# Diagonal blocks of a delta-rule inverse: copied by ScalarE in the first chunk, turned on chip instead of through DRAM in the second

## The chip, the cores and the metric

The kernel runs on one core of a Trainium2 chip. A core has five engines that run side by side, each with its own list of instructions in a fixed order: TensorE (PE in the profile; its weight loads are PEld), VectorE (DVE), ScalarE (ACT), GpSimd (POOL) and SyncE (SP), which here only issues DMA transfers. Engines wait for one another through semaphores. Work tiles lie in an on-chip memory of 128 partitions; TensorE writes its results to eight accumulator banks, and another engine has to copy them out before a bank can be used again. The metric is the time of one execution on the device in microseconds (us).

## The reference

Two blocks are computed one after the other. The first is a delta rule over a sequence, for 4 batches and 8 heads of 768 tokens with a head size of 48: a state matrix is read by each query and then corrected by each key. The second is a feed-forward layer with a SiLU.

```python
k_n = k / (norm(k) + 1e-6)
for t in range(S):                       # S = 768, per batch and head
    y[t] = q[t] @ state                  # state is 48 x 48
    v_old = k_n[t] @ state
    state = state + beta[t] * outer(k_n[t], v[t] - v_old)
x = y as (3072 tokens, 384)
out = silu(x @ w_in) @ w_out             # 384 -> 2048 -> 384
```

## The kernel before

**Chunks.** The 768 tokens are cut into six chunks of 128. Within a chunk the corrections depend on one another through the products of keys with keys. The kernel solves this triangular system by an inverse: the scores (key by key products, tile `ap`) are made by TensorE in `score`; their 32x32 diagonal blocks (four row groups of 32 tokens, 32 batch-head pairs) are brought into a layout where every partition holds one whole block, are inverted there by VectorE step by step (`invert_first` for chunk 0, `invert` for the others, which yield after each rank step), and the inverted blocks are joined to 64x64 ones by small matmuls (`joins` with `corner`, `turned`, `straight` and `merge_half` for chunk 0; `merge` for the others). Then `keys`, `inner`, `old`, `update` and `new` carry the state over the chunk and give the outputs, `hidden` and `combine` (or `project` for chunk 0) are the feed-forward layer.

**How the blocks get into that layout.** Three things have to be there before an inverse starts: the blocks, turned, in a tile `g`; a start value `x`; and a step size for each token, the product of beta and the squared inverse key norm with a minus sign, turned in the same way (`step`).
- Chunk 0: `diagonal_blocks` (line 1304) copies the 32x32 blocks out of the scores into the tile `stage`, eight copies of 32 partitions by 512 numbers, four for each pair of batches g; six are by GpSimd, two by ScalarE (lines 1324 and 1327). VectorE then turns all of them with one transpose (line 1353). The step sizes come out of `norm_steps` (line 395) on VectorE, which turns them with one small transpose as well.
- Chunk 1: `block_out` (line 578) writes the blocks to DRAM, four DMAs for each pair of batches, and `block_in` (line 589) reads them back in the turned layout with one DMA. The step sizes go through a sparse tile `spread` that four VectorE instructions fill (line 430); `block_steps` (line 450) turns it with a matmul on TensorE, and ScalarE copies the result out.
- Chunks 2 to 5 go as chunk 1.

**What sets the order.** No scheduler reorders anything: `pin` ties every instruction behind the one before it on the same engine, in the order of the program text, and `in_line` does this for the DMAs on SP. For chunk 0 the text itself is the order: key turns and scores (`first_score`), block copies, `beta_of(0)` (beta turned by TensorE, copied by ScalarE), query turns (`turn`, whose copies `kq` ScalarE makes), `norm_steps(0)`, query scores (`first_queries`), and filler matmuls (`busy`, line 347) in between, some of which wait for a rank step of the inverse. From the second half of chunk 0's joins on a string of letters is the order (`script`): `r` runs a piece of the feed-forward layer, `s` a step of the solving chain, `l` a step of chunk 1's key lengths, `norm_steps(1)` included, `p` a step of `prepare(1)` (scores and blocks of chunk 1), `g` the step sizes of chunk 1 and the start of its inverse, `i` a rank step, `f` a step of converting weights. Accumulator banks are handed out in three rotating groups, so the order also sets who waits for which bank.

Of the kernel before, what the change touches and what calls it, by code (L numbers as in the profile page):

```python
# [19 lines left out]
def kernel(  # L20
# [374 lines left out]
    def norm_steps(c):  # L395

        seed, t, r = (small.tile([P, BH], kind, name=name, bufs=1)[:] for name, kind in (
            ("seed", U32), ("nt", FP32), ("nr", FP32)
        ))
        ss = sums.pop(c)  # L400
        n = small.tile([P, BH], FP32, name="n", bufs=1)
        by_slot = small.tile([P, 2, B * NP], FP32, name="n_slot", bufs=1)
        yield pin(nc.vector.tensor_scalar(
            out=seed, in0=ss.bitcast(U32), scalar1=-0.5, scalar2=1597463007.0,
            op0=ALU.mult, op1=ALU.add,
        ))
        root = seed.bitcast(FP32)
        for _ in range(3):
            yield pin(nc.vector.scalar_tensor_tensor(
                out=t, in0=ss, scalar=-0.5, in1=root, op0=ALU.mult, op1=ALU.mult  # L410
            ))
            yield pin(nc.vector.tensor_tensor(out=t, in0=t, in1=root, op=ALU.mult))
# [7 lines left out]
        yield pin(nc.vector.tensor_tensor(out=t, in0=r, in1=beta_tok[:, c, :], op=ALU.mult))  # L420
        if c == 0:
            size = small.tile([P, T], FP32, name="step")
            pin(nc.vector.scalar_tensor_tensor(
                out=t, in0=r, scalar=-1.0, in1=t, op0=ALU.mult, op1=ALU.mult
            ))
            pin(nc.vector.transpose(out=size[:], in_=t))
            step_of[0] = size
        for j in range(NB if c > 0 else 0):
            rows = slice(T * j, T * (j + 1))
            yield pin(nc.vector.scalar_tensor_tensor(  # L430
                out=spread[rows, place(c, j), :], in0=r[rows], scalar=-1.0, in1=t[rows],
                op0=ALU.mult, op1=ALU.mult,
            ))
# [123 lines left out]
    def by_pool(to, of):  # L557
        return pin(nc.gpsimd.tensor_copy(out=to, in_=of))  # L558

    blocks = {}  # L560

    def block_room(c):

        if c == 0:
            g, x = (sum_room[:, at : at + T * T] for at in (AT_G, AT_X))
        else:
            g = work.tile([P, T * T], FP32, name="g", tag="g", bufs=1)[:]
            x = (
                sum_room[:, AT_LAST : AT_LAST + T * T] if c == 1
                else work.tile([P, T * T], FP32, name="x", tag="x", bufs=1)[:]  # L570
            )
        pin(nc.gpsimd.memset(x, 0.0))
# [3 lines left out]
        blocks[c] = (tc.dram_tile([P, T, T], FP32, name=f"blocks{c}") if c > 0 else None, g, x)  # L576

    def block_out(c, g):

# [719 lines left out]

        score(0, b, (0,), (A, CC), evacuate)  # L1300

    diagonal = stage[:, 0 : BH * T].rearrange("p (n t) -> p n t", t=T)

    def diagonal_blocks(g, engines):

        for j, by in enumerate(engines):
            rows, cols = slice(T * j, T * (j + 1)), slice(T * (j % 2), T * (j % 2 + 1))
            by(diagonal[rows, HH * g : HH * (g + 1)], aps[0, g][0][rows].rearrange("s u h t -> s (u h) t")[:, :, cols])

    load_q(0, slice(HB, B))  # L1310
    busy(3)
    for b in range(B):
# [32 lines left out]
    for _ in norm_steps(0):  # L1345
# [7 lines left out]
    pin(nc.vector.transpose(  # L1353
        out=blocks[0][1].rearrange("p s t -> p t s"), in_=diagonal.rearrange("p n t -> p t n")
    ))
    for t in xis:
        pin(nc.gpsimd.memset(t, 0.0))
    for c in range(1, NCH):
# [110 lines left out]
    def prepare(c):  # L1469

        def evacuate(j, e, to, of):
            if j == 1:
                mask(to, of)
            else:
                by_act(to, of)

        def scored(b):
            if b == 0:
                block_room(c)
            score(c, b, (0, 1), (A, CC), evacuate)  # L1480
            if b % HB == 1:
                block_out(c, b // HB)

        if in_blocks(c):
            for g in range(2):
                size(c, g)
            if c == 2:
                for b in range(B):
                    turn(c, b, 0, (A, CC)[b % 2], True)
            for g in range(2):  # L1490
                for b in range(HB * g, HB * (g + 1)):
                    turn_blocks(c, b, 1)
                if g == 1:
                    for b in range(HB):
                        scored(b)
                yield
            for b in range(HB, B):
                scored(b)
            block_in(c)
            yield  # L1500
            return
        block_room(1)
        for b in range(B):
            score(1, b, (0,), (CC, CC), evacuate)
# [25 lines left out]
    def script(text):  # L1530

        nonlocal pieces
        for word in text.split():
# [18 lines left out]
            elif what == "p":  # L1552
                go(ready, n)
            elif what == "w":
                paced(fetch_w_out, n)
            elif what == "W":
                paced(fetch_w_in, n)
            elif what == "Q":
                paced(load_q, 1)
            elif what == "o":  # L1560
                busy(n)
            elif what == "u":
                busy(n, wide=NARROW)
            elif what == "h":
                size_half(1, pins[seen_on])
            elif what == "v":
                paced(load_v, 1)
            elif what == "k":
                load_k(2)
            elif what == "g":  # L1570
                step = block_steps(1)
                pin(nc.gpsimd.memset(spread[:], 0.0))
                later["inv"] = invert(1, step)
            elif what == "i":
                go(later["inv"], n)
            elif what == "d":
                flush()
            elif what == "V":
                load_v(2)
            elif what == "G":  # L1580
                load_blocks(q, 2, slice(HB, B))
            elif what == "z":
                size(1, sizes_1.pop(0))
            elif what == "t":
                until(("out", NWI - 1))
                go(sums_made, n)
            elif what == "m":
# [5 lines left out]
    for text in (  # L1593
        "s f3 s q q s j32 b j20 r f j8 q f j4 f j16 r j44 b j4 q j4 r f r j22 f j12 f j8 f b j8 f j4 r j20 e r f j99 h f r f2 l s l r l p r l f p l s l2 f r3 l3 p l s l4 p l2 s r l f l4 f l f l2 p l s l2 s p f r f r l r l2 g i p l p f i p f l i r2 i r v f i3 r3 i r i r i3 b r2 f2 r2 i r2 i2 r2 i f b i r i3 f2 r2 f r3 f i2 r f i f r3 f r f i f i2 r i r i k i2 b z r2 i r i r z r i r2 b r t s r b r f s r2 t s m r m t2 r b m f t m s f b r m2 b m f s r m r s m4 s m3 c m4 s r t G m r2 m4 V m s r m r m t2",
    ):
        script(text)
    for c in range(1, NCH):
# [62 lines left out]
```

## Time and profile before

| | |
|---|---|
| median of 3 runs | 640.37 us (639.87 to 640.62) |
| the profiled execution | 638.56 us, of which the span from first to last instruction is 636.8 |
| busy share of the span: TensorE, VectorE, ScalarE, GpSimd | 97%, 63%, 34%, 15% |
| granted TensorE clock, mean over the span | 0.989 |
| SP's block writes of chunk 1 (issues) | 73.4 to 83.0 us |
| start of the inverse: chunk 0, chunk 1 | 20.0 us, 92.2 us |

Rows of the timeline begin with the start in us from the beginning of the span and the duration in us; then come engine, line, operation, what is written and what is read, with shapes and a count of merged instructions. In square brackets stands the idle time of the engine just before, and what ended it. Rows of a table of stretches give for each stretch its length, each engine's busy time with the number of its instructions, then the granted TensorE clock, the share of the DMA engines that was busy, and GB/s. A row of a DMA queue gives packets, MB and the share of 16 engines' time.

### The profile page before, as it was taken

To read this page: it belongs to the slowest core of one execution; us is meant where nothing else is said; L and a number is where in the kernel's file an instruction comes from. 1 tells how busy PE (TensorE), PEld (TensorE's weight loads), DVE (VectorE), ACT (ScalarE), POOL (GpSimd) and SP (SyncE) were. 2 spreads that over 40 slices of the span, in tenths; PEclk is the share of its full clock that TensorE was granted. 3 is DMA by queue.
4 is the path that set the end of the run, shared out by engine and by line. 5 is a ranking of instruction groups with operands and counts; after the bars stand their busy time and mean duration, and the time that the engine had idled before them with its cause. 6 is when DMAs were issued, how large, how long until landed. Compare 5 with 4: busy or idle time off the path is not lost.

```text
span 636.8 us, 21379 instructions
## 1 busy us (share of the span) xinstructions
PE 620.8 (97%) x9406; PEld 545.9 (86%) x9406; DVE 398.3 (63%) x901; ACT 216.1 (34%) x502; POOL 94.7 (15%) x104
## 2 busy tenths in 40 slices
PE   7879989999999999999999999999999999999997
PEld 5578778666799989989989989989989989889997
DVE  6986779999667974537974546974455964112112
ACT  4457663432441112541122541112451122441110
POOL 6224721335020020020020020020002000000000
PEclk9959999999999999999999999999999999999999
DMA  9646626350459360559150469150353133010101
GB/s 174 132 130 190 202 66 149 107 93 3 100 100 183 63 108 4 110 92 192 26 103 9 97 119 169 35 100 13 75 108 74 26 75 36 18 37 1 26 0 26
DMA packets 141308, 53.65 MB, mean 84 GB/s; under 512 B 112912, under 2 KB 134672, under 8 KB 141216
## 3 DMA queue, kind: packets, MB, share of 16 engines
q1 hardware_dynamic: 140880, 52.14, 39.8%
q8 instruction: 74, 1.21, 0.9%
q10 hardware_dynamic: 336, 0.15, 0.1%
q14 instruction: 18, 0.15, 0.1%
HBM read 39.62 MB, written 10.49 MB: 79 GB/s over the span
## 4 chain that ended last, share of the span: by engine, by line
PE 94%; DVE 3%; issue 1%; DMA 1%; ACT 0%; SPq 0%; POOL 0%; POOLq 0%; DVEq 0%
PE phid L1052 40%; PE px L1169 17%; PE py L1169 13%; PE po L1096 5%; PE pb_c L846 3%; PE pa L537 3%; PE pb_c L834 2%; PE pyc L925 2%; PE pb_c L1096 2%; PE pb_c L866 2%; PE pyc L912 1%; PE px L788 1%; PE py L788 1%; PE pb_c L537 1%; PE pt L508 1%
## 5 line engine op out<-in xcount | busy, mean ns | idle before, releaser
L1052 PE MATMUL phid<-xT,w_in 128*128 128x256 f32 x1152 | 257.1, 381 | 0.2 <-DVE xT L899 0.2
L1052 PEld LDWEIGHTS phid<-xT,w_in 128*128 128x128 f32 x1152 | 216.4, 190 | 30.2 <-issue 0.9
L1062 ACT ACTIVATE gT<-phid 128x512 f32<-128x512 f32 x88 | 52.5, 597 | 145.4 <-PE phid L1052 140.8
L1150 DVE TENSOR_TENSOR sums_of_g<-gT 128x384 f32<-128x384 f32 (+1 forms) x60 | 30.2, 526 | 65.2 <-ACT gT L1062 54.8
L636 DVE SCALAR_TENSOR_TENSOR rank<-g,step,x 128x31 f32<-128x31 f32 (+15 forms) x124 | 49.8, 402 | 22.3 <-DMA g<-blocks 18.8
L1169 PE MATMUL px<-sums_of_w,sums_of_g 128*128 128x192 f32 x320 | 56.6, 329 | 0.0
L1169 PE MATMUL py<-w_out,sums_of_g 128*128 128x192 f32 x320 | 56.2, 328 | 0.0
L1169 PEld LDWEIGHTS py<-w_out,sums_of_g 128*128 128x128 f32 x320 | 52.3, 190 | 0.3
L1169 PEld LDWEIGHTS px<-sums_of_w,sums_of_g 128*128 128x128 f32 x320 | 52.2, 190 | 0.4
L641 DVE TENSOR_TENSOR x<-x,rank 128x31 f32<-128x31 f32 (+15 forms) x124 | 42.5, 343 | 4.3
L475 POOL TENSOR_TENSOR vf<-vf,n_slot 128x768 f32<-128x768 f32 x10 | 14.8, 1493 | 175.5 <-DMA vf<-in_v_dram 175.4
L552 ACT COPY xT<-pyc 48x128 f32<-48x128 f32 (+2 forms) x126 | 32.8, 260 | 1.7
L496 DVE STREAM_TRANSPOSE kq<-stage 128x512 f32<-128x512 f32 x28 | 28.3, 1113 | 4.2 <-DMA xT<-part 2.4
L1169 PE MATMUL py<-w_out,gT 128*128 128x192 f32 x160 | 28.9, 330 | 0.0
L1180 DVE TENSOR_TENSOR o<-o,kept 128x192 f32<-128x192 f32 (+1 forms) x29 | 11.4, 420 | 26.6 <-ACT kept L1177 26.6
L1169 PE MATMUL px<-w_out,gT 128*128 128x192 f32 x160 | 27.9, 327 | 0.0
L1169 PE MATMUL px<-sums_of_w,gT 128*128 128x192 f32 x160 | 27.8, 327 | 0.0
L558 POOL COPY g<-x 64x256 f32<-64x256 f32 x4 | 5.0, 1241 | 150.2 <-DVE x L644 150.2
L1169 PEld LDWEIGHTS px<-w_out,gT 128*128 128x128 f32 x160 | 26.5, 190 | 0.6
L871 DVE TENSOR_TENSOR state<-state,pb_c 128x384 f32<-128x384 f32 x22 | 11.2, 550 | 25.0 <-PE pb_c L866 24.9
L1169 PEld LDWEIGHTS py<-w_out,gT 128*128 128x128 f32 x160 | 26.0, 190 | 0.4
L1169 PEld LDWEIGHTS px<-sums_of_w,gT 128*128 128x128 f32 x160 | 26.2, 190 | 0.1
(228 smaller groups left out, 936.1 us busy)
## 6 DMA issues: line engine op xcount, KB each, us to landing
vf<-in_v_dram SPq DMA_DIRECT2D x48, 96.0 KB, 2.9
out_dram<-o SPq DMA_DIRECT2D x42, 96.0 KB, 2.2
w_out<-in_moe_w_in_dram SPq DMA_DIRECT2D x4, 768.0 KB, 4.9
sums_of_w<-in_moe_w_out_dram SPq DMA_DIRECT2D x4, 768.0 KB, 5.4
blocks<-ap SPq DMA_DIRECT2D x40, 64.0 KB, 1.9
g<-blocks SPq DMA_DIRECT2D x5, 512.0 KB, 3.9
kb<-in_k_dram SPq DMA_DIRECT2D x12, 192.0 KB, 4.3
kb<-in_k_dram SPq DMA_DIRECT2D x24, 96.0 KB, 4.0
```

The costliest lines, as they stand in the source:

```text
L475: pin(nc.gpsimd.tensor_tensor(out=vf, in0=vf, in1=of, op=ALU.mult))
L496: pin(nc.vector.transpose(out=kqs[c, b][:, :, j, :].rearrange("p a (i m) -> p a m i", i=T), in_=src.rearrange("p a (m d) -> p a m d", d=D) ...
L537: pin(nc.tensor.matmul(pa[e][half, p * n * W : (p + 1) * n * W], lhsT=kq[rows, p, 0, half], rhs=kq[rows, p, js[0] : js[-1] + 1, half], sta ...
L552: return pin(nc.scalar.copy(to, of))
L636: pin(nc.vector.scalar_tensor_tensor(out=tv, in0=g[:, 0:m, m : m + 1].to_broadcast([P, m, n]), scalar=step[:, m : m + 1], in1=x[:, m : m + ...
L641: yield pin(nc.vector.tensor_tensor(out=x[:, 0:m, m:T], in0=x[:, 0:m, m:T], in1=tv, op=ALU.add))
L846: yield pin(nc.tensor.matmul(pz[rows, n * D : (n + 1) * D], lhsT=xis[g][rows, u * H + 2 * p + e, :], rhs=vfs[c][rows, hf, g * HB + u, p, : ...
L1052: pin(nc.tensor.matmul(ph[:, j * GT : (j + 1) * GT], lhsT=w_in[:, a, (2 * f + j) * P : (2 * f + j + 1) * P], rhs=xTs[c, hf][:, a, :], star ...
L1062: pin(nc.scalar.activation(out=hidden_of(c, hf, f), in_=ph[:], func=ACTF.Silu, scale=-0.5 if in_blocks(c) else 0.5))
L1096: pin(nc.tensor.matmul(pos[i][:, 0:DM], lhsT=hidden_of(0, hf, f // 2)[:, at : at + C], rhs=w_outs[f // HFF][:, f % HFF, :], start=(f == 0) ...
L1150: pin(nc.vector.tensor_tensor(out=sums_of_g[:, k, fs], in0=of[0], in1=of[1], op=op))
L1169: pin(nc.tensor.matmul(to, lhsT=at, rhs=quarter(f, *b) if isinstance(b, tuple) else sums_of_w[b][:, f], start=start and f == 0, stop=f == ...
```

## The change

1. **Chunk 0.** `diagonal_blocks` takes the chunk as an argument. The copies of the first pair of batches now stand behind all four scores rather than behind the second. Of the eight copies GpSimd makes two and ScalarE six. The transpose is in a function `turn_diagonal`, and stands where it stood.
2. **Chunk 1, blocks.** `diagonal_blocks` copies chunk 1's blocks as well, into the first part of the tile of weight sums (`sum_room`), six copies by ScalarE and two by GpSimd, where the DMAs to DRAM were; `turn_diagonal(1)` turns them with one VectorE transpose where the DMA back was. The DRAM tile of chunk 1 is not made.
3. **Chunk 1, step sizes.** `norm_steps(1)` makes them as `norm_steps(0)` does: one instruction over all partitions and one small transpose in place of four into `spread`; two empty yields keep the number of steps at four. The matmul, the copy on ScalarE and the clearing of `spread` by GpSimd go. An unread matmul into the same bank takes the matmul's place.
4. **Order.** One `p` of the string moves: the query scores of the first batch of chunk 1 now stand behind a stretch of the feed-forward layer (nine matmuls) and right ahead of `g`.

Chunks 2 to 5 are as before.

```diff
         yield pin(nc.vector.tensor_tensor(out=t, in0=r, in1=beta_tok[:, c, :], op=ALU.mult))
-        if c == 0:
-            size = small.tile([P, T], FP32, name="step")
-            pin(nc.vector.scalar_tensor_tensor(
+        if c < 2:
+            step_of[c] = small.tile([P, T], FP32, name="step")
+            yield pin(nc.vector.scalar_tensor_tensor(
                 out=t, in0=r, scalar=-1.0, in1=t, op0=ALU.mult, op1=ALU.mult
             ))
-            pin(nc.vector.transpose(out=size[:], in_=t))
-            step_of[0] = size
-        for j in range(NB if c > 0 else 0):
+            yield pin(nc.vector.transpose(out=step_of[c][:], in_=t))
+            if c == 1:
+                yield
+                yield
+        for j in range(NB if c > 1 else 0):
...
+    def diagonal_blocks(c, g, engines):
+
+        if g == 0:
+            room = stage if c == 0 else sum_room
+            diagonals[c] = room[:, 0 : BH * T].rearrange("p (n t) -> p n t", t=T)
+        for j, by in enumerate(engines):
+            rows, cols = slice(T * j, T * (j + 1)), slice(T * (j % 2), T * (j % 2 + 1))
+            by(
+                diagonals[c][rows, HH * g : HH * (g + 1)],
+                aps[c, g][0][rows].rearrange("s u h t -> s (u h) t")[:, :, cols],
+            )
+
+    def turn_diagonal(c):
+
+        pin(nc.vector.transpose(
+            out=blocks[c][1].rearrange("p s t -> p t s"), in_=diagonals.pop(c).rearrange("p n t -> p t n")
+        ))
...
     first_score(1)
-    diagonal_blocks(0, (by_pool, by_pool, by_pool, by_pool))
     first_score(2)
     first_score(3)
-    diagonal_blocks(1, (by_pool, by_pool, by_act, by_act))
+    diagonal_blocks(0, 0, (by_pool, by_pool, by_act, by_act))
+    diagonal_blocks(0, 1, (by_act, by_act, by_act, by_act))
     add_squares(0, B - 1)
     beta_of(0)
...
             score(1, b, (0,), (CC, CC), evacuate)
             if b % HB == 1:
-                block_out(1, b // HB)
+                diagonal_blocks(1, b // HB, (by_act, by_act) * 2 if b == 1 else (by_pool, by_act) * 2)
             yield
-        block_in(1)
+        turn_diagonal(1)
...
             elif what == "g":
-                step = block_steps(1)
-                pin(nc.gpsimd.memset(spread[:], 0.0))
-                later["inv"] = invert(1, step)
+                unread = bank(A, "pg")
+                pin(nc.tensor.matmul(unread[:, 0:T], lhsT=ident[:], rhs=pick[:], start=True, stop=True))
+                later["inv"] = invert(1, step_of[1])
...
-        "... p l s l2 s p f r f r l r l2 g i p l p ...",
+        "... p l s l2 s f r f r l r l2 p g i p l p ...",
```

More of the change, by code (lines that the diff above doesn't have):

```diff
@@ L558, in by_pool @@
         return pin(nc.gpsimd.tensor_copy(out=to, in_=of))
-    blocks = {}
+    blocks, diagonals = {}, {}
+    def diagonal_blocks(c, g, engines):
[12 more added lines that the diff above has]
+        ))
     def block_room(c):
@@ L575, in block_room @@
         g, x = (t.rearrange("p (s t) -> p s t", t=T) for t in (g, x))
-        blocks[c] = (tc.dram_tile([P, T, T], FP32, name=f"blocks{c}") if c > 0 else None, g, x)
+        blocks[c] = (tc.dram_tile([P, T, T], FP32, name=f"blocks{c}") if c > 1 else None, g, x)
     def block_out(c, g):
@@ L1300, in first_score @@
         score(0, b, (0,), (A, CC), evacuate)
[L1302 to L1308, printed above, removed]
     load_q(0, slice(HB, B))
@@ L1352 @@
     pin(nc.gpsimd.tensor_copy(out=of_step, in_=step[:]))
-    pin(nc.vector.transpose(
-        out=blocks[0][1].rearrange("p s t -> p t s"), in_=diagonal.rearrange("p n t -> p t n")
-    ))
+    turn_diagonal(0)
     for t in xis:
@@ L1593 @@
     for text in (
-        "s f3 s q q s j32 b j20 r f j8 q f j4 f j16 r j44 b j4 q j4 r f r j22 f j12 f j8 f b j8 f j4 r j20 e r f j99 h f r f2 l s l r l p r l f p l s l2 f r3 l3 p l s l4 p l2 s r l f l4 f l f l2 p l s l2 s p f r f r l r l2 g i p l p f i p f l i r2 i r v f i3 r3 i r i r i3 b r2 f2 r2 i r2 i2 r2 i f b i r i3 f2 r2 f r3 f i2 r f i f r3 f r f i f i2 r i r i k i2 b z r2 i r i r z r i r2 b r t s r b r f s r2 t s m r m t2 r b m f t m s f b r m2 b m f s r m r s m4 s m3 c m4 s r t G m r2 m4 V m s r m r m t2",
+        "s f3 s q q s j32 b j20 r f j8 q f j4 f j16 r j44 b j4 q j4 r f r j22 f j12 f j8 f b j8 f j4 r j20 e r f j99 h f r f2 l s l r l p r l f p l s l2 f r3 l3 p l s l4 p l2 s r l f l4 f l f l2 p l s l2 s f r f r l r l2 p g i p l p f i p f l i r2 i r v f i3 r3 i r i r i3 b r2 f2 r2 i r2 i2 r2 i f b i r i3 f2 r2 f r3 f i2 r f i f r3 f r f i f i2 r i r i k i2 b z r2 i r i r z r i r2 b r t s r b r f s r2 t s m r m t2 r b m f t m s f b r m2 b m f s r m r s m4 s m3 c m4 s r t G m r2 m4 V m s r m r m t2",
     ):
```

## The prediction

> **What bounds the kernel now.** I read the page first, then a table of stretches, then the timeline of each engine from 9 to 48 us and from 70 to 95 us, where the edits lie.
>
> ```profile
> PE 620.8 (97%) x9406; PEld 545.9 (86%) x9406; DVE 398.3 (63%) x901; ACT 216.1 (34%) x502; POOL 94.7 (15%) x104
> PE 94%; DVE 3%; issue 1%; DMA 1%; ACT 0%; SPq 0%; POOL 0%; POOLq 0%; DVEq 0%
> ```
>
> ```profile
> core 0: us, PE busy (x) PEld busy (x) DVE busy (x) ACT busy (x) POOL busy (x), PEclk, DMA share, GB/s
> 0.00:34.00 34.00, 27.24 (x518) 18.71 (x520) 26.48 (x74) 16.70 (x37) 16.17 (x40) 1.00 0.77 143
> 34.00:47.70 13.70, 10.94 (x396) 10.48 (x389) 11.09 (x21) 6.43 (x15) 3.11 (x2) 0.50 0.56 151
> 86.60:141.00 54.40, 54.36 (x329) 39.77 (x329) 48.93 (x87) 20.25 (x35) 15.43 (x10) 1.00 0.49 116
> 141.00:636.80 495.80, 491.54 (x7078) 446.69 (x7076) 282.58 (x660) 145.83 (x367) 40.26 (x40) 1.00 0.35 68
> ```
>
> TensorE is the bound (97%, and 94% of the chain that ended last). It is full after 86.6 us; its idle time lies in the first 48 us, where chunk 0's inverse is made, plus one hole of 1.58 us at 85 us. So an edit can move the end only by moving TensorE before 48 us, by closing that hole, or by making TensorE late. In the second row of stretches the granted clock is 0.50 for 13.7 us: TensorE's light stretch costs clock too.
>
> Chunk 0's stage, ScalarE, VectorE and GpSimd:
>
> ```profile
> 12.25 1.24 ACT L552 COPY stage<-ap 32x512 f32<-32x512 f32 x2 [0.19 <-DVE ap L555]
> 13.52 0.20 ACT L364 ACTIVATE beta_tok<-pb 128x32 f32<-128x32 f32 x1
> 13.61 1.08 ACT L518 ACTIVATE kq<-pt 128x512 f32<-128x512 f32 x2
> ```
>
> ```profile
> 12.87 0.48 DVE L409 SCALAR_TENSOR_TENSOR nt<-ss,seed 128x32 f32<-128x32 f32 x1
> 13.39 0.62 DVE L412 TENSOR_TENSOR nt<-nt,seed 128x32 f32<-128x32 f32 x1
> 15.34 0.19 DVE L412 TENSOR_TENSOR nt<-nt,nr 128x32 f32<-128x32 f32 x1
> 17.38 0.23 DVE L420 TENSOR_TENSOR nt<-nr,beta_tok 128x32 f32<-128x32 f32 x1
> 18.00 1.94 DVE L1353 STREAM_TRANSPOSE sums_of_w<-stage 128x1024 f32<-128x1024 f32 x1
> 30.36 1.95 DVE L700 STREAM_TRANSPOSE sums_of_w<-sums_of_w 128x1024 f32<-128x1024 f32 x1
> 32.18 0.32 DVE L730 SCALAR_TENSOR_TENSOR sums_of_w<-pl,second,pick 64x128 f32<-64x128 f32 x1
> 32.91 0.34 DVE L730 SCALAR_TENSOR_TENSOR sums_of_w<-pl,second,pick 64x128 f32<-64x128 f32 x1
> 11.36 3.90 POOL L558 COPY stage<-ap 32x512 f32<-32x512 f32 x6
> ```
>
> TensorE beside them:
>
> ```profile
> 12.67 0.81 PE L347 MATMUL pb_c<-state,ident 128*128 128x384 f32 x2
> 14.26 0.27 PE L537 MATMUL pa<-kq 48*64 48x64 f32 x1 [0.77 <-ACT kq L518]
> 26.23 1.04 PE L508 MATMUL pt<-ident,kb 128*128 128x128 f32 x8
> 27.51 0.66 PE L508 MATMUL pt<-ident,kb 128*128 128x128 f32 x4 [0.24 <-ACT stage L522]
> 29.48 0.91 PE L347 MATMUL pb_c<-state,ident 128*128 128x384 f32 x2 [1.31 <-DVE sums_of_w L689]
> 30.75 0.20 PE L723 MATMUL pl<-sums_of_w,ap 32*32 32x16 f32 x2
> 14.26:26.23 11.97, 11.33 (x161) 7.26 (x162) 10.73 (x34) 6.39 (x18) 3.91 (x11) 1.00 1.00 196
> ```
>
> The reader is to see: VectorE works almost without a break from 12.87 to 33 us and ends the chain here; while GpSimd copies, VectorE's two-input steps take 0.6 us instead of 0.19; but TensorE, too, is nearly full from 14.26 on (11.33 of 11.97 us), and it started at 14.26 because it waited for ScalarE's kq.
>
> **Chunk 0, VectorE's side.** Four block copies leave GpSimd. Six took 3.90 us, so the two that stay end at 11.36 + 1.30 = 12.66. The slowed steps from 12.87 to 15.30 (0.48, then three at the 0.62 of the row at 13.39) become 0.19 each: 0.29 + 3 x 0.43 = 1.58 us saved. Step L420 needs beta_tok, which ScalarE makes behind the copies: four more copies at 0.62 (1.24 for two) are 2.48 us, less the 0.19 us wait that vanishes, so +2.29, and beta_tok ends at 13.72 + 2.29 = 16.01. VectorE would be at L420 at 15.80; it waits 0.2 us. The turn starts 1.35 us earlier, at 16.65, and the last rank step ends at about 28.05 instead of 29.4, where the filler that waits for it starts at 29.48.
>
> **Chunk 0, TensorE's side.** The same 2.29 us stand in front of kq (L518), and behind kq stand the query scores and all that TensorE has in order until the corners. TensorE's first score goes from 14.26 to 16.55; its idle time before it grows from 0.77 to 3.06 us (from 13.48, the end of the filler at 12.67). From there it needs between 11.33 us (all waits gone) and 11.97 us to the turn at 26.23, so that one starts at 27.9 to 28.5; 1.94 us later (28.17 - 26.23) it is at the filler of L347, at 29.8 to 30.5, with no wait for VectorE left. Before it was there at 29.48. So TensorE takes VectorE's place as the late one: the corners (L723) start 0.3 to 1.0 us later, though their operand is ready 1.35 us earlier. Cover: before, VectorE was in its transpose until 32.31 and took the corners' results (L730) at 32.18 and 32.91 with no wait ahead of them, so they lay ready and some of the lateness vanishes there. Against that, TensorE stands idle in the joins behind for nothing that the profile shows (issue), as at the hole at 85 us; if what it waits for is its own instructions, such waits move along with its position. Their rows, the instruction queue of the DMA view from 83 to 87.5 us, and that queue over the whole span:
>
> ```profile
> 40.69 0.21 PE L812 MATMUL pb_c<-xi,xe_y 32*32 32x32 f32 x1 [1.36 <-issue]
> 86.53 0.27 PE L925 MATMUL pyc<-ap,z 64*64 64x64 f32 x1 [1.58 <-issue]
> q8 instruction: 1, 0.02, 2.0%
> q8 instruction: 74, 1.21, 0.9%
> ```
>
> Ends: 0 and +1.0 us; I take +0.5, the 0.65 in the middle of 0.3 to 1.0, less a little cover. VectorE's 1.35 us are worth nothing: TensorE is late next.
>
> **Chunk 1, blocks.** SP loses eight issues of 64 KB and one of 512 KB. ScalarE gets six copies, GpSimd two, VectorE one 1.94 us turn.
>
> ```profile
> 72.70 0.65 ACT L552 COPY ap<-pb_c 128x256 f32<-128x256 f32 x2 [1.48 <-PE pb_c L537]
> 75.80 0.60 ACT L1062 ACTIVATE gT<-phid 128x512 f32<-128x512 f32 x1 [0.72 <-PE phid L1052]
> 78.39 0.60 ACT L1062 ACTIVATE gT<-phid 128x512 f32<-128x512 f32 x1 [1.99 <-PE phid L1052]
> 81.69 0.48 ACT L552 COPY z<-pb_c 128x384 f32<-128x384 f32 x1 [0.59 <-PE pb_c L846]
> 81.58 1.56 PE L1052 MATMUL phid<-xT,w_in 128*128 128x256 f32 x6
> 83.07 0.94 PE L866 MATMUL pb_c<-z,kb 64*48 64x48 f32 x64
> 73.38 9.66 SPq L106 DMA_DIRECT2D blocks<-ap  x8
> 92.16 0.27 DVE L636 SCALAR_TENSOR_TENSOR rank<-g,step,sums_of_w 128x31 f32<-128x31 f32 x1 [2.66 <-ACT step L458]
> ```
>
> Four copies after 73.35 (2.48 us) push the first gT by some 1.9 us; ScalarE's idle 0.72 and 1.99 us take that in before the second gT, whose phid bank TensorE wants no earlier than 81.58. Two more (1.24 us) after the last score's copies, less the idle 0.59, push z from 81.69 to 82.35; it ends at 82.83, TensorE asks at 83.07. Cost 0, with 0.24 us of slack; if that is gone, it costs up to the 0.65 us. GpSimd's two copies (1.3 us) end before its add waits for VectorE anyway. On VectorE four spread steps become one plus a small transpose, and the turn adds 1.94 us ahead of the state adds. The first rank step (92.16) waited 2.66 us for the step sizes from TensorE and ScalarE, a wait that goes; but the masks of score 0 now stand before it, and that score runs behind nine matmuls of the hidden layer, about 4 us later than before. So the inverse starts near 92 us as before. Even a start 1 us either way reaches nothing: between 86.6 and 141 us TensorE had 0.04 us idle.
> The unread matmul replaces the step-size matmul one for one; a copy on ScalarE and a memset on GpSimd go, off the path.
>
> **Chunk 1, the hole at 85 us.** The one instruction packet around it took 2.0% of 16 engines over 4.5 us, 1.44 us, against a mean of 1.24 us over all 74 (0.9% of 16 engines over 636.8 us, by 74). SP issued blocks from 73.38 to 83.04, so their packets shared the engines then; without them I take the difference, -0.2 us. Ends: 0, and the whole 1.58 us.
>
> **Sum.** +0.5 - 0.2 = +0.3 us on the profiled execution's 638.56 (span 636.8). That stands 1.81 us below the median of the runs, 640.37; so 640.37 + 0.3 = 640.7 us.
>
> **Rivals.**
> 1. *The clock falls in chunk 0* (slower). TensorE's idle stretch grows to 3.06 us. Before, the clock fell at 34.0 after a stretch with light 32-row matmuls, and did not fall at 30.58 after 3.41 us with 1.55 idle:
>
> ```profile
> 27.17:30.58 3.41, 1.86 (x11) 1.21 (x10) 3.10 (x11) 1.36 (x3) 0.63 (x1) 1.00 0.05 10
> 42.43:47.65 5.22, 5.22 (x118) 5.10 (x115) 4.92 (x9) 1.55 (x4) 0.00 (x0) 0.50 0.44 82
> ```
>
> It came back after 5.22 us of full work, in which half is lost: 2.6 us at most. Dense fillers follow the idle stretch here, so I take two thirds, 1.8: 642.5 us. It decides if the clock falls at all before 20 us. For it: 3.06 idle is twice the 1.55 that passed. Against: one stretch between dense ones. [...]
> 2. *The gain comes through* (faster). Either the hole at 85 us closes wholly (-1.58, with chunk 0 at no cost: 638.8), or TensorE's fillers give way and VectorE's 1.35 us reach the joins (639.0). Against: TensorE's order is fixed and 11.33 us of it are work.
> 3. *ScalarE's copies hold TensorE in chunk 1.* If a copy takes 1 us instead of 0.62, z is 2 x 0.38 later, the slack of 0.24 is gone and TensorE waits 0.5 us, the gT bank as much again: 641.7 us.
>
> **How the numbers follow.** The forecast (TensorE late by under a microsecond, clock kept) 0.50; rival 1 0.27; rival 2 0.14; rival 3 0.09. A measurement here tells 0.2%, 1.28 us, from no change: same is 639.1 to 641.65. The forecast's own range is 639.8 to 641.6 (its terms' ends without the whole hole) and counts as same but for 0.04; rival 1 is slower, rival 2 faster, rival 3 half and half. So faster 0.14, same 0.50, slower 0.36. Range 639.0 to 643.0: it leaves out the far half of rival 2 and the tail of rival 1.
>
> **What would show it.** In the changed profile: ScalarE's six stage copies in one run from 12.1 to 15.8; TensorE's first query score at about 16.5 after 3 us idle; VectorE's steps at 0.19 from 13 us and its turn at 16.7; no wait of the L347 filler for the last rank step; corners near 31.2; granted clock 1.00 until 34. No blocks issues between 70 and 90 us, a hole of about 1.4 us still there, the first rank step near 92. Wrong would make me: half clock before 30 us, the corners before 30, or TensorE waiting for z or a phid bank at 81 to 84.

## The result and the profile after

The changed kernel takes 641.36 us (median; 639.61 to 642.92) beside 639.6 us of the kernel before: ratio 1.0027, 95% interval 1.0017 to 1.0037, which is +1.1 to +2.4 us. It is slower, for the interval lies above 1, but by little: the prediction took 0.2% as the least difference that a measurement here tells from none, and the interval's lower end lies under that. The profiled execution took 641.09 us (span 638.9), 2.53 us more than that of before.

Two rows of the page of the changed kernel: the granted clock in forty slices, and the chain that ended last.

```profile
PEclk9779999999999999999999999999999999999999
PE 95%; ACT 1%; issue 1%; DMA 1%; DVE 0%; SPq 0%; POOL 0%; POOLq 0%
```

VectorE's share of the chain fell from 3% to 0 and ScalarE got 1%. The slices of about 16 us show the clock below full in the second slice as well as the third; before, it was the third alone.

ScalarE, VectorE, GpSimd and TensorE in chunk 0, from the timeline of the changed kernel, one fence for each engine:

```profile
11.79 3.76 ACT L554 COPY stage<-ap 32x512 f32<-32x512 f32 x6
15.58 0.20 ACT L364 ACTIVATE beta_tok<-pb 128x32 f32<-128x32 f32 x1
15.67 1.08 ACT L520 ACTIVATE kq<-pt 128x512 f32<-128x512 f32 x2
```

```profile
12.80 0.19 DVE L412 TENSOR_TENSOR nt<-nt,seed 128x32 f32<-128x32 f32 x1
15.81 0.19 DVE L420 TENSOR_TENSOR nt<-nr,beta_tok 128x32 f32<-128x32 f32 x1 [0.41 <-ACT beta_tok L364]
16.42 1.94 DVE L578 STREAM_TRANSPOSE sums_of_w<-stage 128x1024 f32<-128x1024 f32 x1
34.58 0.34 DVE L750 SCALAR_TENSOR_TENSOR sums_of_w<-pl,second,pick 64x128 f32<-64x128 f32 x1 [3.87 <-PE pb_c L743]
```

```profile
11.06 1.26 POOL L560 COPY stage<-ap 32x512 f32<-32x512 f32 x2 [0.18 <-DVE ap L557]
```

```profile
12.38 0.81 PE L347 MATMUL pb_c<-state,ident 128*128 128x384 f32 x2
16.32 0.36 PE L539 MATMUL pa<-kq 48*64 48x64 f32 x1 [3.13 <-ACT kq L520]
17.38 4.21 PE L347 MATMUL pb_c<-state,ident 128*128 128x384 f32 x6
32.65 0.81 PE L347 MATMUL pb_c<-state,ident 128*128 128x384 f32 x2
33.83 0.20 PE L743 MATMUL pl<-sums_of_w,ap 32*32 32x16 f32 x2
```

VectorE's side went as the change has it: steps at 0.19 us, the turn at 16.42 instead of 18.00. But VectorE then waits 3.87 us at L750 for TensorE's corners, for which it never waited before. TensorE stood 3.13 us before the first query score, and its fillers behind it (L347 at 17.38) took 4.21 us for six. The same six took 2.20 us in the kernel before:

```profile
14.88 2.20 PE L347 MATMUL pb_c<-state,ident 128*128 128x384 f32 x6
```

The corners run at 33.83 instead of 30.75, and the filler ahead of them, at 32.65, has no wait for VectorE left.

The table of stretches shows what the clock did. The first two stretches are those around the idle time, the third lies in the joins of chunk 0.

```profile
core 0: us, PE busy (x) PEld busy (x) DVE busy (x) ACT busy (x) POOL busy (x), PEclk, DMA share, GB/s
12.16:15.57 3.41, 1.03 (x6) 0.41 (x4) 2.80 (x14) 3.32 (x6) 0.55 (x4) 1.00 1.10 288
15.57:22.40 6.83, 6.08 (x70) 3.68 (x70) 6.00 (x17) 1.82 (x5) 2.56 (x7) 0.50 0.91 191
39.47:49.71 10.24, 9.02 (x300) 8.82 (x300) 7.88 (x15) 4.83 (x10) 1.84 (x1) 0.50 0.54 145
```

TensorE's granted clock is 0.50 from 15.57 to 22.40 us, where it was 1.00 before. Later it is 0.50 from 39.47 for 10.24 us; before, from 33.99 for 13.65. These lengths are two, three and four times 3.41 us; a window here is such a stretch of 3.41 us. To see what the half clock cost, take the same stretch of TensorE's work in both kernels, from the first query score to the corners. The first fence is the kernel before, the second the changed one (length, TensorE busy, clock):

```profile
14.26:30.75 16.49, 14.30 (x179) 1.00 0.77 152
```

```profile
16.32:33.83 17.51, 16.60 (x179) 0.83 0.56 117
```

The same instructions keep TensorE busy for 2.30 us longer. So the corners' delay of 3.08 us adds up: the first score is 2.06 us later (16.32 against 14.26), the half clock costs 2.30, and the wait for VectorE, 1.31 us in the prediction's row at 29.48, is gone: 2.06 + 2.30 - 1.31 = 3.05. In the joins 0.7 us of it come back in this execution, for the second stretch at half clock begins later there and is shorter. TensorE is 2.35 us late at 51 us by its matmul records, 2.13 behind the hole at 88 us, and 2.35 at its last matmul. The profiled execution is not alone in this: the mean granted clock over all executions is 0.9875 for the changed kernel and 0.9892 for the kernel before (beside experiment 1). Over 640 us the difference is as much as 1.1 us without any clock, or 2.2 us more at half clock.

The joins' part is not the same in every execution. The changed kernel was profiled a second time, beside experiment 3. There the clock was at half for one window less in chunk 0 (3.41 us, from 17.46 to 20.87) and for one more in the joins (13.65 us):

```profile
37.94:51.59 13.65, 10.89 (x308) 0.50 0.58 157
```

Its corners were 2.45 us late (33.20), and TensorE was 3.29 us late at 51 us: here the joins added 0.84 us. In the kernel of experiment 1 that has chunk 0 as before, the joins' half clock was 10.24 us long, and TensorE was 0.94 us early at 51 us. So a difference of less than about 1 us at 51 us in a single trace shows nothing by itself.

Chunk 1's stage in the changed kernel: ScalarE, GpSimd and VectorE first, then TensorE.

```profile
75.76 2.50 ACT L554 COPY sums_of_w<-ap 32x512 f32<-32x512 f32 x4
83.51 1.24 ACT L554 COPY sums_of_w<-ap 32x512 f32<-32x512 f32 x2
84.78 0.48 ACT L554 COPY z<-pb_c 128x384 f32<-128x384 f32 x1
83.54 2.06 POOL L560 COPY sums_of_w<-ap 32x512 f32<-32x512 f32 x2 [3.01 <-ACT ap L554]
94.36 0.26 DVE L656 SCALAR_TENSOR_TENSOR rank<-g,step,sums_of_w 128x31 f32<-128x31 f32 x1
```

```profile
85.45 0.94 PE L886 MATMUL pb_c<-z,kb 64*48 64x48 f32 x64
88.67 0.27 PE L945 MATMUL pyc<-ap,z 64*64 64x64 f32 x1 [1.33 <-issue]
```

All of it lies about 2.35 us later than before. ScalarE's z ends at 85.26 and TensorE's matmuls take it (L886) at 85.45, with the same shift as ahead of them; the first rank step starts at 94.36, which is 92.0 plus the shift, and the hole is 1.33 us instead of 1.58.

### The profile page after: what moved, and what is told of

Same layout as the page of the kernel before. It is cut to its first block, busy times and chain, and to the rows that moved or that the text cites. A ratio compares the mean times of both kernels' runs of the same rounds, so it can differ in the third digit from the quotient of the medians.

```text
span 638.9 us, 21371 instructions
## 1 busy us (share of the span) xinstructions
PE 621.8 (97%) x9406; PEld 546.5 (86%) x9406; DVE 396.8 (62%) x900; ACT 222.2 (35%) x511; POOL 94.0 (15%) x101
## 3 DMA queue, kind: packets, MB, share of 16 engines
q8 instruction: 74, 1.21, 0.8%
## 4 chain that ended last, share of the span: by engine, by line
PE 95%; ACT 1%; issue 1%; DMA 1%; DVE 0%; SPq 0%; POOL 0%; POOLq 0%
PE phid L1072 40%; PE px L1189 17%; PE py L1189 13%; PE po L1116 5%; PE pa L539 3%; PE pb_c L866 3%; PE pb_c L854 2%; PE pyc L945 2%; PE pb_c L1116 2%; PE pb_c L886 1%; PE pyc L932 1%; PE pb_c L347 1%; PE px L808 1%; PE py L808 1%; PE pt L510 1%
```

## The experiments

In the short diffs the lines are those of the kernel from which the experiment starts. All the kernels compute the whole reference; added fillers are matmuls whose results nothing reads. Times "against before" are ratios to runs of the kernel before on the same chip, beside them.

**1. Chunk 0's copies alone, and the rest alone.** The first kernel is the one before with chunk 0's new split of the copies, the second the changed one with chunk 0's copies as they were.

```diff
 # chunk0_only, from the kernel before
-    diagonal_blocks(0, (by_pool, by_pool, by_pool, by_pool))
...
-    diagonal_blocks(1, (by_pool, by_pool, by_act, by_act))
+    diagonal_blocks(0, (by_pool, by_pool, by_act, by_act))
+    diagonal_blocks(1, (by_act, by_act, by_act, by_act))
 # chunk1_only, from the changed kernel
+    diagonal_blocks(0, 0, (by_pool, by_pool, by_pool, by_pool))
...
-    diagonal_blocks(0, 0, (by_pool, by_pool, by_act, by_act))
-    diagonal_blocks(0, 1, (by_act, by_act, by_act, by_act))
+    diagonal_blocks(0, 1, (by_pool, by_pool, by_act, by_act))
```

> Only chunk 0's copies change: two by GpSimd, six by ScalarE, behind all four scores; chunk 1 goes through DRAM as before. Theory (the changed kernel loses in chunk 0, because ScalarE's copies hold kq back, TensorE stands idle for 3.1 us and the clock falls at once): the whole loss is here, +1.6 to +2.4 us against before, first query score at 16.3, half clock before 25 us, corners at 33 to 34 us. Rival (chunk 1's six ScalarE copies and the turn cost something): +0.5 to +1.2 us here, the rest in the other half.

> Only chunk 1's blocks and step sizes change; chunk 0 as before. Theory (chunk 0 carries the loss): -0.3 to 0 us, the hole at 85 us shrinks from 1.58 to about 1.3 us, no new wait of TensorE. Rival (chunk 1 costs): +0.5 to +1.5 us, with a wait of TensorE for ScalarE's z or for a bank at 75 to 85 us.

Chunk 0's copies alone: 641.32 us against 638.67, ratio 1.0029 (1.0012 to 1.0046). The rest alone: 638.76, ratio 0.9992 (0.9978 to 1.0006). So no loss outside chunk 0 shows. The loss of the first kernel was forecast at +1.6 to +2.4 us; by the ratio it is +0.8 to +2.9. Its profiled execution took 639.03 us, 2.29 under its median, and its last matmul is only 0.5 us late: its rows show the fall of the clock, not the whole loss. Of the first kernel, TensorE's first query score and the same stretch as above:

```profile
16.48 0.27 PE L537 MATMUL pa<-kq 48*64 48x64 f32 x1 [3.12 <-ACT kq L518]
18.02:21.43 3.41, 3.41 (x37) 0.50 0.79 178
16.48:32.75 16.27, 15.36 (x180) 0.90 0.61 125
```

Of the second, the score, the stretch and the hole:

```profile
14.02 0.27 PE L539 MATMUL pa<-kq 48*64 48x64 f32 x1 [0.77 <-ACT kq L520]
14.02:30.49 16.47, 14.30 (x179) 1.00 0.81 154
84.97 0.27 PE L945 MATMUL pyc<-ap,z 64*64 64x64 f32 x1 [0.96 <-issue]
```

With the idle stretch of 3.12 us the clock falls again, here for one window of 3.41 us instead of two, and the stretch costs 15.36 - 14.30 = 1.06 us more. The corners are at 32.75; 33 to 34 was forecast. With 0.77 us idle it doesn't fall, and the stretch costs what it did. In chunk 1 the hole shrinks to 0.96 us in this execution (about 1.3 was forecast) and TensorE has no new wait.

**2. The same copies, but kq first.** Chunk 0 gives GpSimd three copies; ScalarE makes two ahead of kq and its last three behind the first batch's query scores. The new argument `first` tells `diagonal_blocks` with which of the four row groups to begin.

```diff
-    def diagonal_blocks(c, g, engines):
+    def diagonal_blocks(c, g, engines, first=0):
...
     diagonal_blocks(0, 0, (by_pool, by_pool, by_act, by_act))
-    diagonal_blocks(0, 1, (by_act, by_act, by_act, by_act))
+    diagonal_blocks(0, 1, (by_pool,))
...
     first_queries(0)
+    diagonal_blocks(0, 1, (by_act, by_act, by_act), 1)
     busy(3)
```

> The changed kernel, but ScalarE makes only two copies ahead of kq, GpSimd makes a third one, and ScalarE's last three stand behind the copies of the first query scores. Theory: TensorE's first query score at about 13.9 us, its idle time there 0.6 us, clock 1.00 until the joins, VectorE's turn at about 16.7 us instead of 18.0, corners at 29.4 to 30 us, -0.7 to -1.5 us against before. Rival (VectorE's earlier turn is worth nothing, because TensorE or its instruction stream sets the start of the joins anyway): corners at 30.5 to 31, -0.4 to +0.3 us.

Measured 638.28 us against 638.67: ratio 0.9991 (0.9977 to 1.0004), and the loss is gone. The gain of 0.7 to 1.5 us that was expected is not shown: the interval, -1.5 to +0.3 us, holds it and the rival's -0.4 to +0.3 alike. From its trace, the first score, the wait for VectorE's last rank step, and the stretch:

```profile
13.83 0.27 PE L539 MATMUL pa<-kq 48*64 48x64 f32 x1 [0.61 <-ACT kq L520]
28.73 0.91 PE L347 MATMUL pb_c<-state,ident 128*128 128x384 f32 x2 [1.28 <-DVE sums_of_w L709]
13.83:30.01 16.18, 14.04 (x179) 1.00 0.83 165
```

The clock stays at 1.00, VectorE ends the chain again, and the corners, at 30.01, are 0.74 us earlier than before, where the theory had 29.4 to 30 and the rival 30.5 to 31. What cost time was where the copies stood ahead of kq, not that ScalarE made more of them. This kernel removes the idle stretch and the half clock together, so it doesn't weigh the one against the other; the busy time of the stretch does.

**3. The idle stretch filled, by moving fillers.** The three fillers between the query scores of batches 0 and 1 run ahead of the first ones. TensorE gets no instruction more and ScalarE's copies stay where the change put them.

```diff
-    busy(1)
+    busy(4)
     for _ in norm_steps(0):
         pass
     first_queries(0)
-    busy(3)
     first_queries(1)
```

> The changed kernel with the same number of TensorE instructions: busy(1) ahead of the norm steps of chunk 0 becomes busy(4), and the busy(3) between the queries of batch 0 and batch 1 goes. So the fillers that ran behind the first query score at 17.4 us (4.21 us in the changed kernel's trace) now run ahead of it, in the stretch in which TensorE had stood for 3.1 us. Clock theory (the loss comes from the half clock at 15.6 us, which the idle stretch sets off): idle ahead of the first query score about 1 us, the clock at 1.00 until about 34, the corners' matmuls at 29.5 to 31 instead of 33.8, TensorE at 51 us no later than in the kernel before, and a time of -1.3 to +0.3 us against it. Count theory (what cost time when the fillers were lengthened was 16 more TensorE instructions): the same -1.3 to +0.3, since none is added here. Lateness theory (ScalarE's four more copies hold up a chain that TensorE waits for anyhow, whatever the clock): corners at 33 or later and +1.5 to +2 us. Hand-over theory (the loss of the lengthened fillers comes from TensorE's own order shifted against the transfers later on, through the start time and not the count): +1 us or more although the clock is kept.

> The same kernel as the one with the fillers moved ahead of the first query score, timed again beside the changed kernel itself, to have both against one set of runs of the kernel before. If its gain over the changed kernel is the half clock and the idle stretch that it avoids, it is 1.5 to 2.5 us faster than the changed kernel, and -1.5 to +0.3 us against before: with the earlier runs that decides whether it beats both.

> The changed kernel itself beside it. By the first comparison +0.17 to +0.37%, which is +1.1 to +2.4 us against before; the profile again with an idle stretch of about 3.1 us ahead of the first query score and the clock at 0.50 for 3.4 or 6.8 us behind it.

Measured 637.31 us against 637.74: ratio 0.9991 (0.9975 to 1.0006). Again, beside the changed kernel itself: 637.3 against 637.9, ratio 0.9992 (0.9975 to 1.0010), while the changed kernel took 640.49, ratio 1.0047 (1.0028 to 1.0066). So moving three fillers takes away the loss, 3.2 us in that comparison, more than the 1.5 to 2.5 expected; the changed kernel itself was 1.8 to 4.2 us slower there, where 1.1 to 2.4 were expected. That it goes holds although kq is as late as in the changed kernel. From the trace of the kernel with the moved fillers (the first of the two):

```profile
12.83 2.75 PE L347 MATMUL pb_c<-state,ident 128*128 128x384 f32 x8
16.76 0.27 PE L539 MATMUL pa<-kq 48*64 48x64 f32 x1 [1.19 <-ACT kq L520]
14.18:17.59 3.41, 2.22 (x57) 1.00 1.08 185
```

From the repeated profile of the changed kernel, the window in which it stood idle, and the stretch:

```profile
14.05:17.46 3.41, 0.62 (x32) 1.00 1.04 183
16.84:33.20 16.36, 15.45 (x180) 0.90 0.57 124
```

The clock stayed at 1.00 past 34 us (1.00 from 17.59 to 34.00, 0.69 from 34.00 to 50.66), and the corners came at 29.67, earlier than the 30.75 of the kernel before, as forecast. So a late kq has no measurable cost by itself: it is TensorE's empty time ahead of it, and the clock that falls behind that, that cost. This kernel, too, takes away both together. The moved fillers beat the changed kernel; against the kernel before, 0.9991 and 0.9992 with intervals that hold 1 are no measurable gain.

**4. Half the dose.** Four copies each for GpSimd and ScalarE in chunk 0.

```diff
-    diagonal_blocks(0, 1, (by_act, by_act, by_act, by_act))
+    diagonal_blocks(0, 1, (by_pool, by_pool, by_act, by_act))
```

> The changed kernel with chunk 0's eight diagonal copies split four to GpSimd and four to ScalarE (before: six and two; changed: two and six). ScalarE has two more copies of 0.62 us ahead of the gates and kq instead of four, so the first query score comes about 1.1 us later than before and TensorE stands there for about 1.9 us. Clock theory: the price is a step, not a slope. If 1.9 us idle keep the clock, TensorE at 51 us is -0.3 to +0.5 us against before and the whole time 0 to +0.4; if they don't, the half clock shows before 20 us for 3.4 or 6.8 us, and the loss is +1.1 or +2.3 us at 51 us. Lateness theory: half of the loss of the changed kernel's copies, +0.8 to +1.0 us, with the clock at 1.00 until the joins.

Measured 638.49 us against 637.74: ratio 1.0013 (0.9995 to 1.0030), which tells none of the theories apart by the time. The trace says more: 1.87 us idle, and the clock fell.

```profile
13.54:16.95 3.41, 1.54 (x36) 1.00 1.14 231
16.95:20.36 3.41, 3.41 (x37) 0.50 0.73 124
15.47:31.78 16.31, 15.39 (x180) 0.90 0.71 135
```

Here too the stretch is 15.39 - 14.30 = 1.09 us longer in busy time, and the corners are 1.03 us late (31.78 against 30.75). At 51 us only 0.43 of it is left: the joins' stretch at half clock is 10.24 us instead of 13.65. The forecast for a fallen clock, at least 1.1 us at 51 us, failed, for it left the joins out.

**5. The idle stretch filled with more fillers.** Four more in place of moved ones; the counted places of the large loads move with the work.

```diff
-    busy(1)
+    busy(5)
...
-    PACKET, WINDOW = 256, 445
+    PACKET, WINDOW = 256, 461
```

> The changed kernel with four more filler matmuls of L347 on TensorE ahead of the first query score (busy(5) in place of busy(1); the anchors of the paced loads are moved by the same count), so that TensorE does not stand idle while ScalarE copies. TensorE is as late as in the changed kernel, only busy. Theory (the clock is the cost): clock 1.00 until the joins, corners at 31 to 31.7 us, 0 to +0.7 us against before. Rival (the lateness itself is the cost): +1.5 to +2.2 us as the changed kernel, corners at 33 us or later.

Measured 642.46 us against 638.67: ratio 1.0049 (1.0032 to 1.0066). The expectation failed for the time, though it held in chunk 0: the first score is as late as in the changed kernel, but TensorE is busy ahead of it, the clock stayed at 1.00 to 37.4 us, the corners came at 31.06, and TensorE was 0.22 us late at 51 us. So this trace tells the clock from the lateness, which experiments 1 to 4 don't: a first score 2.12 us late (16.38 against 14.26) put the corners 0.31 us behind with the clock kept, and one 2.06 us late put them 3.08 us behind with the clock at half. The loss in time came later, at places where TensorE had not stood before. The first score, and the waits of over 0.6 us behind 41 us, from the timeline of this kernel:

```profile
16.38 0.27 PE L539 MATMUL pa<-kq 48*64 48x64 f32 x1 [0.54 <-ACT kq L520]
42.70 0.54 PE L866 MATMUL pb_c<-vf,xi 64*64 64x48 f32 x5 [1.11 <-issue]
57.32 0.18 PE L772 MATMUL pl<-sums_of_w 32*32 32x32 f32 x1 [0.67 <-issue]
83.70 0.20 PE L866 MATMUL pb_c<-vf,xi 64*64 64x48 f32 x1 [1.00 <-issue]
97.18 1.10 PE L1072 MATMUL phid<-xT,w_in 128*128 128x256 f32 x4 [1.87 <-DMA xT<-part]
```

**6. Sixteen instructions more, without the change.** A filler stands in the traces as two matmuls and two weight loads (three of them are the x6 at 14.88 us of the kernel before), four TensorE instructions, so experiment 5 added 16. Three kernels add them to the kernel before, in time in which TensorE waits there, or move the loads, or both. A fourth repeats experiment 5 with the loads left. By the count theory, as in experiment 3, the 16 cost the time by themselves (+1.5 to +3.5 us for `before_shifted`); by the loads theory it is the loads that were moved along; by the work theory, the work that stands 16 instructions later.

```diff
 # before_shifted and before_work: ahead of the filler that waits for the last rank step
+            busy(4, wide=NARROW)
 # before_shifted and before_loads
-    PACKET, WINDOW = 256, 445
+    PACKET, WINDOW = 256, 461
 # filled_in_step, from the changed kernel
-    busy(1)
+    busy(5)
```

> The kernel before with 16 more narrow filler matmuls (busy(4, wide=NARROW)) where TensorE waits for the last rank steps of chunk 0, near 28 us, in time that it would otherwise stand; the list of small loads that is counted by TensorE's instructions is moved by the same 16. Nothing else is changed. [...] If the count is nothing: within 0.4 us all along, and what cost the kernel with longer fillers is its own timing.

> The kernel before with WINDOW 461 instead of 445 and nothing else: eleven large loads (w_in, w_out, chunk 1's q) leave 16 TensorE instructions later, the instructions themselves are as they were. Loads theory (the two kernels with 16 more TensorE instructions lost about 4 us because these loads, whose place is counted in TensorE instructions, were moved by 16 too and now lie on the fetches of TensorE's own instructions): +1.5 to +4 us, with longer gaps of TensorE behind 40 us. [...]

> The kernel before with the 16 added TensorE instructions (four narrow fillers where TensorE waits at 28 us) and WINDOW left at 445, so that the eleven large loads keep their place in the count of instructions while the work behind the fillers moves by 16. Loads theory: within 0.5 us of before. Work theory: +1.5 to +4 us.

> The changed kernel with busy(5) instead of busy(1) ahead of the norm steps of chunk 0, as in the kernel with lengthened fillers, but WINDOW left at 445. Clock theory: TensorE stands for no more than 1 us near 16 us, the clock is 1.00 until the joins, and TensorE at 51 us is -0.5 to +0.7 us against before. With the loads theory on top of it the whole time is then -0.5 to +0.7 us; with the work theory it stays at +2.5 to +4.5 us, as it was with the loads moved along.

| kernel | us, and before beside it | ratio (95%) |
|---|---|---|
| before, 16 more, loads moved along | 641.72, 637.74 | 1.0058 (1.0036 to 1.0079) |
| before, loads moved alone | 640.43, 638.98 | 1.0029 (1.0005 to 1.0053) |
| before, 16 more, loads left | 642.3, 638.98 | 1.0054 (1.0033 to 1.0075) |
| changed, 16 more, loads left | 640.75, 638.98 | 1.0041 (1.0023 to 1.0058) |

Sixteen instructions in time that was idle cost the kernel before about as much as they cost experiment 5, so that experiment's time says nothing against the clock. The added instructions alone cost that much, whatever the change. The work theory holds for the larger part. The fourth kernel lost 1.5 to 3.7 us by its interval (2.5 to 4.5 forecast by this theory, -0.5 to +0.7 by the loads), with the clock at 1.00 to 37.3 us and TensorE 0.24 us late at 51 us, as forecast. The loads moved alone cost 0.3 to 3.4 us; that doesn't decide between the two forecasts for them (+1.5 to +4 us by the loads theory, within 0.5 by the work theory). From the timeline of the kernel before with 16 more and the loads left, waits of over 0.5 us behind 41 us:

```profile
43.11 0.65 PE L846 MATMUL pb_c<-vf,xi 64*64 64x48 f32 x7 [1.11 <-issue]
57.92 0.18 PE L752 MATMUL pl<-sums_of_w 32*32 32x32 f32 x1 [0.96 <-issue]
84.28 0.20 PE L846 MATMUL pb_c<-vf,xi 64*64 64x48 f32 x1 [0.99 <-issue]
88.38 0.38 PE L925 MATMUL pyc<-ap,z 64*64 64x64 f32 x9 [0.58 <-issue]
97.52 0.67 PE L1052 MATMUL phid<-xT,w_in 128*128 128x256 f32 x2 [1.31 <-DMA xT<-part]
```

Four of the five stand at the same work as in experiment 5; the kernel before had one hole of 1.58 us in their place. In the records of the instruction queue's packets (16 KB each: 1.21 MB in 74), each of the four marked "issue" ends 0.5 to 1.5 us behind the end of a packet: 42.64 for the first, then 56.60, 82.90 and 86.92. That speaks for instructions that came late; no run changed these packets alone, so this is the author's reading, and the cost alone is shown.

## Why the prediction was right and wrong

The time lies in the range, but that is partly luck. The change was forecast at +0.3 us and measured at +1.1 to +2.4. The forecast time, 640.7 us, started from 640.37, the median of three runs; the median of before beside the changed kernel is 639.6, so 0.8 us of the closeness to 641.36 come from the starting point. The range was wide enough to hold both the likeliest case and rival 1, at 642.5, and what came about was rival 1, given 0.27.

- **"The clock kept" is the step that failed.** The forecast was a granted clock of 1.00 until 34 us. It was 0.50 from 15.57 us on for 6.83 us. Rival 1 was to decide "if the clock falls at all before 20 us", and it did. Its mechanism and sign are right. Its price was put at 1.8 us, two thirds of 2.6 (which is 1.7); in chunk 0 it measured 2.30 us of TensorE's time with two windows at half clock (6.83 us), and 1.06, 1.09 and 1.15 with one (3.41 us).
- **TensorE's side without the clock was right.** Corners later by 0.3 to 1.0 us were forecast, 0.5 taken. Measured 3.08, less the clock's 2.30, is 0.78. The first score came at 16.32 (16.55 forecast) after 3.13 us idle (3.06).
- **VectorE's side was right.** Steps at 0.19 us, a wait of 0.41 for beta_tok (0.2 forecast), the turn at 16.42 (16.65), and TensorE's wait for the last rank step gone. As forecast, the gain was worth nothing, for TensorE was late next; VectorE then waited 3.87 us for the corners.
- **The cover behind the corners was left open by the runs.** A little was forecast. In the first profile 0.7 us of the 3.08 came back, because the joins had one window less at half clock; in the second 0.84 us were added, with as many windows as before. The prediction had no term for the half clock in the joins, which is 10.24 or 13.65 us long from one trace to another where no instruction was added.
- **Chunk 1 at cost 0 was right**, by its own run: 0.9992 with an interval that holds 1. ScalarE's z ends 0.19 us before TensorE takes it (0.24 forecast); the first rank step is in its place once the 2.35 us are taken off. One size was off: GpSimd's two copies took 2.06 us, not 1.3, and nothing waited for them. Rival 3 did not come.
- **The hole at 85 us**: -0.2 forecast, -0.25 measured in the changed kernel (1.58 to 1.33); it was -0.62 where chunk 0 was left as before (0.96). Over the kernels whose chunk 1 no longer goes through DRAM, and that have a hole there, it is 0.68 to 1.33 us, 1.07 in the mean of seven profiles; with DRAM and no instruction added it is 1.43, 1.58 and 1.71. So the sign is right and the size was more like 0.5 us. That the missing transfers are the reason stays argued.
- **Rival 2, the gain coming through**, did not come. The run with kq ahead of the last copies has VectorE's chain a little earlier, and by the corners 0.74 us are gained, of which the end shows 0.9991 and an interval with 1 in it.
- **A sum.** The forecast's own range, 639.8 to 641.6, is wider than its terms give: from 640.37, with 0 to +1.0 for chunk 0 and -0.2 to 0 for the hole, it is 640.2 to 641.4.

The weight between the likeliest case and rival 1 turned on how much of a window TensorE may stand idle before the clock falls. The runs give that now. The windows ahead of a fall below, and those in which the clock was kept, come from the rows of the kernels above, of the prediction, and of the run with the loads moved alone, whose clock also fell once more, behind a wait at 109 us:

```profile
108.68:112.09 3.41, 1.42 (x7) 1.00 0.08 31
112.09:115.50 3.41, 3.41 (x10) 0.50 0.36 77
```

| TensorE busy in a window of 3.41 us | clock in the next |
|---|---|
| 0.62, 1.03, 1.42, 1.54 us | 0.50 |
| 1.65 (experiment 5), 1.86 (before, 27.17 to 30.58), 2.22 us | 1.00 |

The row of experiment 5, around its wait at 97 us:

```profile
95.42:98.83 3.41, 1.65 (x8) 1.00 0.01 1
```

Outside the joins the limit lies between 1.54 and 1.65 us of busy time in these traces, a little under half of the window. In the joins it is another: the fall at 34 us in the kernel before came behind a window of light 32-row matmuls with 2.76 us busy, so busy time alone is not all that counts. In these traces the time at half clock was 3.41 us or a multiple of it (6.83, 10.24, 13.65), and the same kernel lost two windows in chunk 0 in one execution and one in the other. 1.54 us of work in a window did not keep the clock. The chance of 0.27 for rival 1 was the author's estimate; the one such window in the rows of before that ended ahead of the joins, with 1.86 us busy, had kept the clock.

## What to carry to other kernels

Before work is put in front of what TensorE waits for, add up TensorE's idle time there: in this kernel a stretch of 0.77 us cost only itself, while one of 1.9 to 3.1 us halved the clock for the dense work behind it and cost 1.1 to 2.3 us more there. Where such a wait can't be avoided, move filler matmuls that stand behind it to ahead of it, rather than add new ones. Give the engine that feeds TensorE its feeding work first and the copies that only a later transpose needs behind it.

## What the runs showed of the hardware that was not expected

- The clock fell after windows in which TensorE still worked, for up to 1.54 us of 3.41 (45%). With 3.1 us idle it stayed at half for two windows in one execution of the changed kernel (6.83 us), where TensorE was busy for 2.66 us of the first (15.57 to 18.98), and for one in another (3.41), where it was busy throughout (17.46 to 20.87). In the profiles of the kernel before and of the changed one the last window at half clock was a full one each time: 44.23 to 47.64 in the first, 18.98 to 22.40 and 46.30 to 49.71 in the second. A window with 3.14 us busy (changed kernel, 42.88 to 46.30) did not end it, nor did the first of two full ones in the kernel before (40.82 to 44.23).
- Sixteen TensorE instructions more, run in time in which TensorE stood still anyway, made the kernel before 0.33 to 0.79% slower, more than the change that was studied. In one such kernel's trace four waits of 0.58 to 1.11 us, for which the profile shows no releaser, end 0.5 to 1.5 us behind the end of a 16 KB packet of the instruction queue; that the packets are their cause is not shown.
- Eleven large loads that leave 16 instructions later, and nothing else, cost 0.05 to 0.53% in the one comparison made. In its profile TensorE is 0.20 us early until 105 us and loses its time at one place, a wait of 2.08 us for ScalarE that ends at 110.67, with a window at half clock behind it; why is open.
